# Decode block with attention and MLP in parallel: the last seven w2 rows in four column groups, and one add at the end

## The chip, the cores and the metric

The kernel runs on one core of a Trainium2 chip. Such a core has five engines that run side by side: TensorE (PE in the profile; its weight loads are PEld), VectorE (DVE), ScalarE (ACT), GpSimd (POOL) and SyncE (SP), which here only issues DMAs. TensorE writes its results to PSUM, the engines copy them from there to SBUF, and 16 DMA engines move data between SBUF and the chip's main memory (HBM).

The metric is the time of one execution on the device, in microseconds (us). A kernel is run several times and the median counts.

## The reference

Two rows of x (B = 2, one token each, D = 576) are normalised once and go through two branches. Branch A is attention with a key and value cache, 32 query heads on 16 key heads, over the last 2,048 of 8,192 positions. Branch B is an MLP of width F = 4,608 with a squared ReLU. The output is the sum of x and the two.

```python
def _B_ref(x, w1, b1, w2, b2):
    h = jnp.einsum("bsd,df->bsf", x, w1) + b1
    zero = jnp.zeros_like(h)
    r = jnp.where(h > zero, h, zero)
    h = r * r
    out = jnp.einsum("bsf,fd->bsd", h, w2) + b2
    return out

x = A_x
xn = _layernorm(x, axis=-1)
return x + _A_ref(xn, A_k_cache, A_v_cache, A_wq, A_wo) + _B_ref(xn, B_w1, B_b1, B_w2, B_b2)
```

All inputs and the output (2 x 1 x 576) are bf16.

## The kernel before

All large loads go through SP's DMA queue, in the order in which the program issues them: keys and values of eight units (4 key heads of one batch row each), wq in between, then w1, wo in two halves, and at the end w2. The matmuls follow the loads. Per unit TensorE transposes the keys (L281), multiplies them with the queries (L296), and after the softmax multiplies the values (L333).

Everything that adds to the output is summed in one PSUM tile, out_ps, of 34 partitions x 288 columns in f32. Row b of columns 0 to 287 is on partition b, row b of columns 288 to 575 on partition 32 + b. The helper out_acc (L242) makes one contribution: two matmuls with the same 128x2 weights, one for each half, 288 columns each, which write partitions 0 to 1 and 32 to 33. So the two go to two column groups of TensorE's array. x, the bias b2, 64 matmuls of wo, and all rows of w2 go through out_acc.

The "rows" of w2 are chunks of 128 of the 4,608 values of h: a chunk of h (128x2) is the weight, and 128 rows of w2 (128 x 576) stream through. w2 comes in four groups. Groups 0, 1 and 2 have nine such chunks each and one load each. Group 3 has seven chunks (FT = 7) in one tile, loaded in pieces of four, two and one (the list W2P: `(3, 0, 4), (3, 4, 6), (3, 6, 7)`); the rest of that group is in two small tiles loaded early on ACT's queue (w2x_sb, w2y_sb) and done by mlp_x. The function mlp_o(g, r0, r1) runs one entry of W2P.

The order at the end of the program is: values of the last units, wo_sel(1) and wo_acc(1) with the second half of wo, then the six entries of W2P, and then the end proper, which is L502 to L506: DVE casts columns 0 to 143 of out_ps to bf16, ACT columns 144 to 287 (both on 34 partitions), and SP's and ACT's queues each store one half of the columns of both rows, as two pieces of 576 bytes.

The first MLP layer (mlp_h_block, L377) and the query projection (q_block, L259) already use four column groups: the four matmuls of a chunk write partitions 32 g and 32 g + 1 for g = 0 to 3, with `tile_position=(0, 32 * g)`.

PSUM tiles are taken from rings. The ring misc has two buffers and serves, at the end of the program, oT_ps of the last unit, then wps of wo_sel(1). The tile framework puts in the waits between engines from the tiles that they read and write.

Of the kernel before, what the change touches and what calls it, by code (L numbers as in the profile page):

```python
# [8 lines left out]
F32 = mybir.dt.float32  # L9
BF16 = mybir.dt.bfloat16  # L10
ACT = mybir.ActivationFunctionType
ALU = mybir.AluOpType
# [4 lines left out]
def kernel(  # L17
# [14 lines left out]
    nc = tc.nc  # L32
    P = 128
    B, Sq, D = A_x.shape
# [27 lines left out]
    NG4 = 4  # L62
# [5 lines left out]
    FR = HW // P  # L68
    XR, XP, XE = 12, 20, 5
    FT = (HW - XR * XP) // P  # L70
# [6 lines left out]
    NFC = N3 + len(CX)  # L77
    RB = 32 * (NG4 - 1) + B
    OH = D // 2
    NP = NQ // 2  # L80
    WR = 2 * NC * Dh // P
    DW = Dh // WR
# [2 lines left out]
    const = ctx.enter_context(tc.tile_pool(name="const", bufs=1))  # L85
# [5 lines left out]
    work = ctx.enter_context(tc.tile_pool(name="work", bufs=2))  # L91
    keep = ctx.enter_context(tc.tile_pool(name="keep", bufs=3))
    psum = ctx.enter_context(tc.tile_pool(name="psum", bufs=1, space=bass.MemoryType.PSUM))

    x2d = A_x.rearrange("b s d -> (b s) d")
    out2d = out.rearrange("b s d -> (b s) d")

    k_tiles, v_tiles, wq_tiles, w1_tiles, wo_tiles, w2_tiles = {}, {}, {}, {}, {}, {}
# [135 lines left out]
    with nc.allow_low_precision(reason="sums of one 1 and zeros"):  # L234
        nc.vector.tensor_reduce(out=rmask[:], in_=ident[:].rearrange("p (c r) -> p r c", r=WR), axis=AX.X, op=ALU.add)
        nc.vector.tensor_reduce(out=sel[:, MZ:MZ + DW], in_=ident[:].rearrange("p (c r) -> p c r", r=WR), axis=AX.X,
                                op=ALU.add)

    out_ps = psum.tile([32 + B, OH], F32, tag="out", name="out_ps")
    nc.vector.memset(out_ps[:], 0.0)  # L240

    def out_acc(lhsT, rhs_of, start=False, stop=False, pin=False):  # L242
        for i in range(2):
            mm = nc.tensor.matmul(out_ps[32 * i:32 * i + B, :], lhsT=lhsT, rhs=rhs_of(i * OH, (i + 1) * OH),  # L244
                                  start=start, stop=stop, skip_group_check=True)
            if pin:
                tc.keep_in_program_order(mm)
# [111 lines left out]
    def wo_acc(tq):  # L359
        ws = wo_state.pop(tq)  # L360
        wo_sb = wo_tiles.pop(tq)
        for r in range(WR):
            out_acc(ws[:, r, :], lambda a, z: wo_sb[:, r, a:z])

    mlp = {}
# [36 lines left out]
            nc.vector.tensor_copy(out=hT_sb[0:m, N3 + i0:N3 + i1, :], in_=hb[0:m, i0:i1, :])  # L402
        mlp["h"] = hT_sb

    def mlp_o(g, r0, r1, last=False):
        w2_sb = w2_tiles.pop((g, r0))
        for r in range(r0, r1):
            o = (r - r0) * D
            out_acc(mlp["h"][:, g * FR + r, :], lambda a, z: w2_sb[:, o + a:o + z], stop=(last and r == r1 - 1))

    def mlp_x():
        for i, (c0, st, m) in enumerate(CX[FT:]):
# [15 lines left out]
    W2P = [(0, 0, 9), (1, 0, 9), (2, 0, 9), (3, 0, 4), (3, 4, 6), (3, 6, 7)]  # L428
# [23 lines left out]
    for g in range(NG):  # L452
# [7 lines left out]
                          in_=ident[0:NG4, 0:NG4].unsqueeze(2).to_broadcast([NG4, NG4, 32]))  # L460
# [34 lines left out]
        pv(NU - 1, g)  # L495
    wo_sel(1)
    wo_acc(1)
    for i in range(len(W2P)):
        mlp_o(*W2P[i], last=(i == len(W2P) - 1))

    fin_sb = work.tile([32 + B, OH], BF16, tag="fin", name="fin_sb")
    half_o = OH // 2  # L502
    nc.vector.tensor_copy(out=fin_sb[:, 0:half_o], in_=out_ps[:, 0:half_o])  # L503
    nc.scalar.copy(out=fin_sb[:, half_o:OH], in_=out_ps[:, half_o:OH])  # L504
    nc.sync.dma_start(out=out2d[:, 0:OH], in_=fin_sb[0:B, :])
    nc.scalar.dma_start(out=out2d[:, OH:D], in_=fin_sb[32:32 + B, :])  # L506


# [28 lines left out]
```

## Time and profile before

| | |
|---|---|
| median of 8 runs | 136.34 us (136.1 to 137.03) |
| the profiled execution, its own time | 137.03 us |
| its span, first to last instruction | 135.24 us |
| mean granted TensorE clock | 0.785 |
| busy share of the span | PE 76%, PEld 64%, DVE 42%, ACT 33%, POOL 5% |
| HBM read | 53.62 MB, 397 GB/s over the span |
| out_ps matmuls on w2 (L244), 128x288 | 68, of 386 ns mean |
| last casts (L503 DVE, L504 ACT), 34x144 | 300 ns and 273 ns |
| output stores (L505, L506) | 2, of 1.1 KB each |

The first rows of the profile give shares of the whole span. The matmuls' durations overlap, since several are in flight at once; their pace is the distance between their starts. The clock that the profile calls granted is a share of TensorE's full clock and changes during a run, between 0.5 and 1.0 here. A chain of waits follows the work that ended last back through whatever released it. L-numbers are lines of the kernel before.

### The profile page before, as it was taken

The numbers are of one execution on the slowest core, as the hardware profiler recorded it, in microseconds if no ns is written. First come the engines' busy times: TensorE is split into PE (matmuls) and PEld (weight loads), VectorE is DVE, ScalarE is ACT, GpSimd is POOL, SyncE is SP. The second block draws the span as 40 slices with busy tenths as digits, with TensorE's granted clock in tenths as the row PEclk, the third lists the DMA queues.
The fourth block names the chain that finished last, engine by engine and source line by source line (L and its number), as shares of the span: only waits on it lengthen the run. The fifth ranks groups of instructions, "written<-read, shape, count | busy, mean of one in ns | idle before, by whom it ended". The sixth has DMA issues, their size and how long they took to land.

```text
span 135.2 us, 4107 instructions
## 1 busy us (share of the span) xinstructions
PE 103.0 (76%) x1876; PEld 85.9 (64%) x1876; DVE 56.5 (42%) x133; ACT 44.4 (33%) x52; POOL 6.7 (5%) x21
## 2 busy tenths in 40 slices
PE   1072994786998689967979996998948999489491
PEld 0061471686987589867968995984417987445240
DVE  7631030455377358665564457247042456300000
ACT  6723020645466226454253315411040551000000
POOL 1000000011011011011010011011000001100000
PEclk9999999868699855999955555595599599555959
DMA  4999999999999999999999999999999999999930
GB/s 156 426 408 437 429 426 427 422 436 419 435 417 431 409 414 426 422 426 422 431 422 429 419 431 430 420 419 427 413 433 426 426 428 424 415 410 415 382 143 1
DMA packets 4430, 53.87 MB, mean 398 GB/s; under 512 B 527, under 2 KB 678, under 8 KB 1194
## 3 DMA queue, kind: packets, MB, share of 16 engines
q1 hardware_dynamic: 4324, 53.32, 93.6%
q8 instruction: 14, 0.23, 0.7%
q10 hardware_dynamic: 90, 0.31, 0.6%
q14 instruction: 2, 0.02, 0.0%
HBM read 53.62 MB, written 0.00 MB: 397 GB/s over the span
## 4 chain that ended last, share of the span: by engine, by line
PE 36%; DMA 36%; DVE 16%; ACT 4%; POOL 3%; issue 2%; SPq 1%; POOLq 0%; ACTq 0%
DMA w<-in_B_w_dram 23%; PE kT_ps L281 16%; DMA wq<-in_A_wq_dram 9%; PE sc_ps L296 7%; PE out_ps L244 6%; PE oT_ps L333 4%; DMA b_sb<-in_B_b_dram 4%; DVE l L315 3%; DVE sub L310 3%; DVE kT L286 3%; DVE m L302 3%; ACT pT L313 2%; PE q_ps L259 2%; ACT kT L284 2%; POOL gmax L306 1%
## 5 line engine op out<-in xcount | busy, mean ns | idle before, releaser
L281 PE MATMUL kT_ps<-ident,k 128*128 128x128 bf16 x512 | 51.4, 272 | 4.0 <-DVE kT L286 2.5
L281 PEld LDWEIGHTS <-k 128*128 128x128 bf16 x512 | 42.0, 124 | 5.5 <-issue 2.4
L284 ACT COPY kT<-kT_ps 128x1024 bf16<-128x1024 bf16 x32 | 31.8, 1011 | 36.8 <-PE kT_ps L281 35.3
L286 DVE COPY kT<-kT_ps 128x1024 bf16<-128x1024 bf16 x32 | 21.5, 682 | 27.1 <-PE kT_ps L281 26.6
L296 PE MATMUL sc_ps<-qT_all,kT 128*128 128x8 bf16 x512 | 22.1, 169 | 6.5 <-ACT kT L284 3.8
L296 PEld LDWEIGHTS <-kT 128*128 128x128 bf16 x512 | 20.1, 103 | 8.8 <-ACT kT L284 4.9
L333 PE MATMUL oT_ps<-pT,v 128*128 128x8 bf16 x512 | 15.3, 167 | 1.7 <-issue 1.2
L333 PEld LDWEIGHTS <-v 128*128 128x128 bf16 x512 | 14.2, 97 | 2.7 <-issue 2.1
L313 ACT ACTIVATE pT<-sub 128x512 bf16<-128x512 f32 x8 | 5.0, 631 | 20.1 <-DVE sub L310 20.1
L315 DVE TENSOR_REDUCE l<-pT 128x8 f32<-128x512 bf16 x8 | 8.6, 1069 | 3.7 <-ACT pT L313 3.6
L244 PE MATMUL out_ps<-wo,ws 128*2 128x288 bf16 x64 | 8.0, 442 | 1.3 <-DMA wo<-in_A_wo_dram 0.7
L244 PE MATMUL out_ps<-w,hT_sb 128*2 128x288 bf16 x68 | 7.2, 386 | 2.1 <-DMA w<-in_B_w_dram 2.1
L244 PEld LDWEIGHTS <-hT_sb 128*2 128x2 bf16 (+2 forms) x94 | 5.0, 102 | 5.8 <-issue 2.6
L302 DVE TENSOR_REDUCE m<-sc_ps 128x8 f32<-128x512 f32 x8 | 5.5, 692 | 5.4 <-PE sc_ps L296 5.4
L306 POOL PARTITION_ALL_REDUCE gmax<-m x8 | 3.0, 374 | 85.4 <-DVE m L304 85.4
L244 PEld LDWEIGHTS <-ws 128*2 128x2 bf16 x64 | 3.9, 121 | 4.5 <-DVE ws L356 1.2
L504 ACT CAST fin_sb<-out_ps 34x144 bf16<-34x144 f32 x1 | 0.3, 273 | 18.7 <-DVE fin_sb L503 18.7
L503 DVE CAST fin_sb<-out_ps 34x144 bf16<-34x144 f32 x1 | 0.3, 300 | 13.6 <-PE out_ps L244 13.6
L310 DVE TENSOR_TENSOR sub<-sc_ps,gm 128x512 f32<-128x512 f32 x8 | 5.5, 691 | 0.3
L259 PE MATMUL q_ps<-wq,xnT 128*2 128x512 bf16 x32 | 3.4, 482 | 3.0 <-DMA wq<-in_A_wq_dram 3.0
L317 POOL PARTITION_ALL_REDUCE lsum<-l x8 | 3.2, 399 | 23.2 <-DVE l L315 23.2
L387 DVE TENSOR_TENSOR hrow<-t 98x384 bf16<-98x384 f32 x3 | 1.6, 556 | 5.2 <-ACT t L386 5.0
(70 smaller groups left out, 43.8 us busy)
## 6 DMA issues: line engine op xcount, KB each, us to landing
k<-in_A_k_cache_dram SPq DMA_DIRECT2D x8, 2048.0 KB, 12.2
v<-in_A_v_cache_dram SPq DMA_DIRECT2D x8, 2048.0 KB, 25.0
wo<-in_A_wo_dram SPq DMA_DIRECT2D x2, 2304.0 KB
w<-in_B_w_dram SPq DMA_DIRECT2D x2, 2304.0 KB, 32.7
wq<-in_A_wq_dram SPq DMA_DIRECT2D x2, 2048.0 KB, 16.9
w<-in_B_w_dram SPq DMA_DIRECT2D x3, 1296.0 KB, 28.1
w_rem<-in_B_w_dram SPq DMA_DIRECT2D x1, 576.0 KB
w<-in_B_w_dram SPq DMA_DIRECT2D x1, 576.0 KB
```

Of the source, the lines that this page charges most:

```text
L244: mm = nc.tensor.matmul(out_ps[32 * i:32 * i + B, :], lhsT=lhsT, rhs=rhs_of(i * OH, (i + 1) * OH), start=start, stop=stop, skip_group_chec ...
L259: nc.tensor.matmul(q_ps[k][32 * g:32 * g + B, :], lhsT=xnT[:, xc, :], rhs=rhs, start=(c == 0), stop=(c == KC - 1), skip_group_check=True, ...
L281: nc.tensor.transpose(out=kT_ps[:, i * P:(i + 1) * P], in_=k_sb[:, j * Dh:(j + 1) * Dh], identity=ident[:])
L284: nc.scalar.copy(out=kT[:], in_=kT_ps[:])
L286: nc.vector.tensor_copy(out=kT[:], in_=kT_ps[:])
L296: nc.tensor.matmul(sc_ps[:, g * JG + i, :], lhsT=kT[:, i * P:(i + 1) * P], rhs=qT_all[:, b, tq * NC:(tq + 1) * NC], start=True, stop=True)
L302: nc.vector.tensor_reduce(out=m1[:], in_=sc_ps[:].rearrange("p j c -> p c j"), axis=AX.X, op=ALU.max)
L306: nc.gpsimd.partition_all_reduce(gmax[:], m2[:], channels=P, reduce_op=ReduceOp.max)
L310: nc.vector.tensor_tensor(out=sub[:], in0=sc_ps[:], in1=gm2[:].unsqueeze(1).to_broadcast([P, NJ, NC]), op=ALU.subtract)
L313: nc.scalar.activation(out=pT[:], in_=sub[:], func=ACT.Exp, scale=scale)
L315: nc.vector.tensor_reduce(out=l1[:], in_=pT[:].rearrange("p j c -> p c j"), axis=AX.X, op=ALU.add)
L333: nc.tensor.matmul(oT_ps[:], lhsT=v_sb[:, j * Dh:(j + 1) * Dh], rhs=pT_tiles[u][:, j, :], start=(j == 0), stop=(j == NJ - 1))
```

## The change

The first 27 chunks of w2 (groups 0 to 2) still go to out_ps. When the last of them is in, out_ps is copied to an f32 tile in SBUF, part, by four copies of 2x144, two by DVE and two by ACT, that also rearrange it: quarter i of the 576 columns goes to partitions 32 i and 32 i + 1. The last seven chunks go, by four matmuls of 144 columns each, to a new PSUM tile, tail_ps, with the same arrangement, in four column groups. At the end one DVE operation adds tail_ps and part on 98 partitions and writes bf16; the two stores then take one output row each, from four partitions that are 32 apart, in four pieces of 288 bytes.

part is zeroed by POOL at the start; tail_ps takes a buffer of the ring misc and is zeroed by DVE, which the program issues between the last use of DVE in wo_sel(1) and its cast of wps (L356). W2P, the loads and their order are as before.

```diff
+    OQ = D // 4
...
-    def mlp_o(g, r0, r1, last=False):
+    def mlp_o(g, r0, r1):
         w2_sb = w2_tiles.pop((g, r0))
         for r in range(r0, r1):
             o = (r - r0) * D
-            out_acc(mlp["h"][:, g * FR + r, :], lambda a, z: w2_sb[:, o + a:o + z], stop=(last and r == r1 - 1))
+            out_acc(mlp["h"][:, g * FR + r, :], lambda a, z: w2_sb[:, o + a:o + z], stop=(g == NG4 - 2 and r == r1 - 1))
+
+    part = const.tile([RB, OQ], F32, name="part")
+    nc.gpsimd.memset(part[:], 0.0)
+
+    def mlp_tail(r0, r1):
+        w2_sb = w2_tiles.pop((NG4 - 1, r0))
+        if r0 == 0:
+            mlp["out"] = psum.tile([P, OQ], F32, tag="misc", bufs=2, name="tail_ps")
+            nc.vector.memset(mlp["out"][:], 0.0)
+        for r in range(r0, r1):
+            o = (r - r0) * D
+            for i in range(4):
+                nc.tensor.matmul(mlp["out"][32 * i:32 * i + B, :], lhsT=mlp["h"][:, (NG4 - 1) * FR + r, :],
+                                 rhs=w2_sb[:, o + i * OQ:o + (i + 1) * OQ], start=(r == 0), stop=(r == FT - 1),
+                                 skip_group_check=True, tile_position=(0, 32 * i))
...
-    for i in range(len(W2P)):
-        mlp_o(*W2P[i], last=(i == len(W2P) - 1))
-
-    fin_sb = work.tile([32 + B, OH], BF16, tag="fin", name="fin_sb")
-    half_o = OH // 2
-    nc.vector.tensor_copy(out=fin_sb[:, 0:half_o], in_=out_ps[:, 0:half_o])
-    nc.scalar.copy(out=fin_sb[:, half_o:OH], in_=out_ps[:, half_o:OH])
-    nc.sync.dma_start(out=out2d[:, 0:OH], in_=fin_sb[0:B, :])
-    nc.scalar.dma_start(out=out2d[:, OH:D], in_=fin_sb[32:32 + B, :])
+    for w in W2P[:NG4 - 1]:
+        mlp_o(*w)
+    for i in range(4):
+        cp = nc.scalar.copy if i % 2 else nc.vector.tensor_copy
+        cp(out=part[32 * i:32 * i + B, :],
+           in_=out_ps[32 * (i // 2):32 * (i // 2) + B, (i % 2) * OQ:(i % 2 + 1) * OQ])
+    for w in W2P[NG4 - 1:]:
+        mlp_tail(*w[1:])
+
+    fin_sb = work.tile([RB, OQ], BF16, tag="fin", name="fin_sb")
+    nc.vector.tensor_tensor(out=fin_sb[:], in0=mlp["out"][0:RB, :], in1=part[:], op=ALU.add)
+    for b, eng in ((0, nc.sync), (1, nc.scalar)):
+        eng.dma_start(out=out2d[b:b + 1, :].rearrange("o (q n) -> (o q) n", q=4), in_=fin_sb[b:RB:32, :])
```

## The prediction

> **What bounds the kernel now.** I read the slices first, then the DMA share of the queues, then the chain of waits near its end, then the tail's instructions in order of time, then busy time and granted clock by stretch. The slices and the queue list say that the loads set the pace:
>
> ```profile
> PEclk9999999868699855999955555595599599555959
> DMA  4999999999999999999999999999999999999930
> q1 hardware_dynamic: 4324, 53.32, 93.6%
> ```
>
> The DMA row is at nine tenths or more in all but the first and the last two slices. So nothing before the last load can gain anything here; only what comes after the last weights can. The chain of waits shows what that is:
>
> ```profile
> 97.97 30.77 DMA w<-in_B_w_dram
> 128.74 0.04 issue
> 128.78 3.68 PE out_ps L244 x32
> 132.47 0.02 issue
> 132.49 0.31 DVE fin_sb L503
> 132.80 0.02 issue
> 132.82 0.27 ACT fin_sb L504
> ```
>
> One releasing load, then 32 matmuls (16 rows of w2, two each), then two casts one after the other, then the stores. The 16 rows are the nine of w2's third block (its load is the 1.89 us wait below) and the last seven, so the change touches 14 of these 32 matmuls, both casts and both stores. The tail in order of time (start, duration, then the instruction; each line is the first of a narrow window):
>
> ```profile
> 128.78 0.64 PE L244 MATMUL out_ps<-w,hT_sb 128*2 128x288 bf16 x4 [1.89 <-DMA w<-in_B_w_dram]
> 130.65 1.17 PE L244 MATMUL out_ps<-w,hT_sb 128*2 128x288 bf16 x8
> 132.03 0.41 PE L244 MATMUL out_ps<-w,hT_sb 128*2 128x288 bf16 x4
> 133.12 0.33 SPq L505 DMA_DIRECT2D out_dram<-fin_sb  x1
> 128.50:131.90 3.40, 3.12 (x28) 1.70 (x29) 0.00 (x0) 0.00 (x0) 0.00 (x0) 0.51 0.37 143
> 131.90:135.20 3.30, 0.54 (x8) 0.17 (x4) 0.30 (x1) 0.27 (x1) 0.00 (x0) 0.99 0.00 1
> ```
>
> The last two lines are stretches (busy time by engine, then granted clock, DMA share, GB/s): the clock is 0.51 until 131.9 and 0.99 after. In the half-clock part a row starts every 0.24 us, both of its matmuls within 5 ns of each other (288 columns, so 0.83 ns a column, two column groups side by side); at full clock every 0.12 us. The ninth row starts at 130.65, the tail's first at 130.89. The last packet of the last load ends at 130.80 in the packet records.
>
> **The change, part by part.** I count from 130.65 to the moment the stores are issued, now 133.12.
>
> *Tail matmuls.* Removed: 14 of 288 columns, in two groups. Added: 28 of 144 columns, in four groups, each with its weight load. The nearest row is the four-group matmul of the first MLP layer (L377, 128x384), which the trace has at both clocks: at half clock the same group starts again every 0.32 us, which is 384 x 0.83 ns, so four groups run as fast as one; at full clock every 0.16 us. By that a tail row takes 144 x 0.83 = 0.12 us. The floor of issue is lower: L296 (8 columns, a new weight load each) runs at 26.5 ns for a pair of load and matmul at half clock, so four pairs are 0.106 us. The upper bound is one group at a time: 4 x 0.12 = 0.48 us. I take 0.12, as the same form of instruction did it. The seventh row then starts at 130.89 + 6 x 0.12 = 131.61, after its load has landed (130.80), and a matmul lasts 0.444 - 0.24 + 0.12 = 0.324 us, so TensorE ends at 131.94 in place of 132.44.
>
> [...]
>
> *The copies out of out_ps.* These are new: four of 2x144, two on DVE and two on ACT, behind the ninth row's end at 130.65 + 0.444 = 131.10. The rows for them are the casts of 34x144: 0.300 us (DVE L503) and 0.273 us (ACT L504). In the changed program DVE's two copies wait for TensorE alone, while each ACT copy waits for the DVE copy of the same PSUM partitions, as the ACT cast does now. So with a hop of 0.02 to 0.03 us: DVE 131.13 to 131.43 and to 131.73; ACT 131.46 to 131.73 and 131.76 to 132.03. They lie beside the tail matmuls, in another PSUM tile; what of them is not covered is 132.03 - 131.94 = 0.09 us, so they, not TensorE, end last before the add, narrowly. Were all four in a row, they would end at 132.36.
>
> *The last operation.* Two casts in series (0.31 + 0.02 + 0.27 = 0.60 us) go; one DVE add of 98x144 comes, PSUM plus SBUF in f32 to bf16. The rows: the same operation on PSUM and SBUF takes 0.167 us for 8 columns (L338) and 0.691 for 512 (L310), 1.04 ns a column, so 0.31 us for 144. It starts at 132.06, ends at 132.37, and the stores are issued at 132.40: **0.72 us before** 133.12.
>
> *Stores.* Each goes from two pieces of 576 B to four of 288 B; still one on SP's queue and one on ACT's, nothing queued behind either. The present packets last 0.033 to 0.035 us each, the first starting 0.74 us after the issue and the last ending at 133.93; the rest to 135.24 is completion and the program's end. No packet between 88 and 576 B is in the trace. From below: 0.02 us less for a shorter packet. From above: one more trip of the length from issue to first data, 0.74 us, were a small piece read before it is written. I take zero, as the packets are a thirtieth of the 2.1 us and the rest does not depend on their size, and keep 0.74 for the range. [...]
>
> *At no cost.* The memset of part on POOL follows that of sel (128x248, 0.306 us, at 0.72) and has until POOL's first reduction, some 25 us later. The memset of tail_ps (at most 0.30 us by L240, 34x288) comes on DVE between L347, which ends at 118.20, and L356, which starts at 118.70 after waiting 0.49 us for wps. Without that cover ws would be up to 0.3 us later, and TensorE then still waits for wo's load (0.67 us of idle, to 119.33). Its buffer's last reader (L338, 117.58) is done. The 28 added TensorE instructions and 2 on DVE come at the end of their streams and push nothing else.
>
> **Sum.** In the profiled execution 137.03 - 0.72 = 136.31, of which the span is 135.24 and 1.79 lies around it. That execution is the slowest of the eight; the median, 136.34, is 0.69 below, and I subtract 0.7 from it: **135.64**. The difference of the two may be profiling, or clock. So I redo the sum with the clock: with the ninth row's start as zero, a tail all at half clock issues its stores at 7 x 0.24 + 0.444 + 0.68 = 2.80 now and 0.444 + 1.31 = 1.75 after, a gain of 1.05; one all at full clock at 0.84 + 0.287 + 0.68 = 1.81 now and 0.287 + 1.31 = 1.60 after, a gain of 0.2. The half-clock stretch began after the 1.89 us idle, which the median execution has too, so I stay with the mixed case and take these two as the likeliest case's own range: 135.3 to 136.14.
>
> **The rivals.**
> - *A warm tail.* Where the clock is full for the last rows, the matmuls saved are worth half as much and the copies, not TensorE, set the add. Gain 0.2 to 0.4, so 135.95 to 136.14. For it: the median is faster than the profiled execution, and full clock already came at 131.9. Against: the idle time ahead of it.
> - *The small stores pay another trip*: 135.64 + 0.74 = 136.38, no change. For it: no such packet is in the trace. Against: two packets of 576 B show no sign of a cost by size.
> - *The column groups do not run side by side for such short matmuls* (slower). The place is the seven tail rows. At 0.48 us a row the fourth matmul of the last row starts at 130.89 + 6 x 0.48 + 0.36 = 134.13 and ends at 134.45, the stores go at 134.81, 1.69 us later than now: 138.0. It decides from the pace at which the add would end where the casts end now, at 133.09: TensorE at 132.75, so 6.75 r + 0.324 = 1.86 after 130.89, r = 0.23 us a row. For it: four weight loads in 0.12 us have no row with a stream this short (a load lasts 0.126 us at half clock). Against: L377 overlaps the loads of all four groups with the streams.
> - *The edit changes nothing*, because the copies come late in their queues: in the changed program they stand directly behind ws on DVE and the last exp on ACT, both idle since before 120, so I give it nothing of its own.
>
> **How the numbers follow.** A measurement of this kernel tells about 0.3% (0.41 us) from no change. The forecast with a gain above 0.41 has 0.62; the warm tail 0.18, within 0.41; the stores 0.12, two thirds within 0.41 and the rest slower, where a warm tail adds to them; the serial groups 0.08, slower. So faster 0.62, same 0.26, slower 0.12. The range 135.3 to 136.4 takes in the forecast, the warm tail and the stores' plain case, and leaves out the serial groups, the part of the stores' case that is slower, and a little below.
>
> **What would show it.** Right: tail matmuls that start again in their group every 0.12 us at half clock, the last one ending some 0.8 us after the ninth row's; DVE copies of 0.30 us beside them; the add waiting for ACT's second copy, by under 0.1 us, and lasting 0.31 us; stores 1.7 us after the ninth row's start; 2.1 us from there to the end. Wrong: an add that waits for TensorE with a tail pace above 0.2 us, copies all in a row, or more than 2.3 us from issue to end. The prediction falls if the stores' end grows by over 0.7 us, or the clock in the tail is full in most executions.

## The result and the profile after

The changed kernel takes 135.48 us (median of 22 runs, 135.23 to 136.39) against 136.26 us (60 runs): a ratio of 0.9941, 95% interval 0.9927 to 0.9955, so 0.78 us faster. The forecast was 135.64. The time is right, and the working that led to it is mostly not, as the profile already hints. The profiled execution took 135.54 us, and its span is 133.6. First the same rows of the page as before: granted clock, DMA share, and the queue of the large loads.

```profile
PEclk9999999855699955999959959955955589658997
DMA  4999999999999999999999999999999999999950
q1 hardware_dynamic: 4328, 53.32, 94.2%
```

The same 53.32 MB arrive, but the share of the span is larger. The end of the chain of waits:

```profile
107.92 22.21 DMA w<-in_B_w_dram
130.14 0.04 issue
130.18 0.26 PE tail_ps L423 x4
130.44 0.03 issue
130.47 0.02 DVEq L524
130.49 0.04 issue
130.53 0.31 DVE fin_sb L524
```

Here the chain waits for the *last* load, and a single row (four matmuls) is left after it. Before, it waited for the load of w2's third block and did 16 rows after it. The tail in order of time, with what ended the idle time in brackets:

```profile
127.74 1.27 PE L245 MATMUL out_ps<-w,hT_sb 128*2 128x288 bf16 x18 [1.84 <-DMA w<-in_B_w_dram]
129.04 0.63 DVE L518 COPY part<-out_ps 2x144 f32<-2x144 f32 x2 [10.81 <-PE out_ps L245]
129.12 0.42 PE L423 MATMUL tail_ps<-w,hT_sb 128*2 128x144 bf16 x16
129.43 0.56 ACT L518 COPY part<-out_ps 2x144 f32<-2x144 f32 x2 [15.37 <-DVE part L518]
129.82 0.59 PE L423 MATMUL tail_ps<-w,hT_sb 128*2 128x144 bf16 x12 [0.28 <-DMA w<-in_B_w_dram]
130.53 0.31 DVE L524 TENSOR_TENSOR fin_sb<-tail_ps,part 98x144 bf16<-98x144 f32 x1 [0.86 <-PE tail_ps L423]
130.87 0.66 SPq L526 DMA_DIRECT2D out_dram<-fin_sb  x1
130.88 0.59 ACTq L526 DMA_DIRECT2D out_dram<-fin_sb  x1
127.00:130.20 3.20, 2.00 (x46) 1.21 (x45) 0.60 (x2) 0.54 (x2) 0.00 (x0) 1.00 0.53 210
```

Three readings differ from the forecast. The tail ran at full clock (1.00 in the stretch of the last line, third number from the end), nine rows of w2 in 1.27 us, and then waited for loads. The two stores take twice as long to issue, 0.66 and 0.59 us in place of 0.33 and 0.26. And everything is about a microsecond earlier: the nine rows start at 127.74, not 128.78. Since their start is the end of a load, that last point has nothing to do with the tail. The load stream itself is faster, which stretches of the run show (the last two columns are the DMA engines' share and GB/s). Before:

```profile
30.00:60.00 30.00, 25.38 (x576) 24.53 (x576) 17.78 (x35) 14.10 (x17) 2.30 (x6) 0.83 1.01 423
90.00:120.00 30.00, 24.15 (x487) 18.89 (x488) 12.08 (x31) 6.67 (x9) 1.53 (x4) 0.74 1.00 421
```

After:

```profile
30.00:60.00 30.00, 25.47 (x576) 24.55 (x576) 17.87 (x35) 14.12 (x17) 2.30 (x6) 0.79 1.01 429
90.00:120.00 30.00, 24.00 (x429) 18.12 (x427) 10.08 (x25) 6.04 (x8) 1.17 (x3) 0.67 1.00 426
```

The share is full in both, so no gap was closed; the same busy engines move about 1% more. In the packet records the last load packet ends at 129.78 after and at 130.79 before.

### The profile page after: what moved, and what is told of

Same layout as the page of the kernel before. It is cut to its first block, busy times and chain, and to the rows that moved or that the text cites. A ratio compares the mean times of both kernels' runs of the same rounds, so it can differ in the third digit from the quotient of the medians.

```text
span 133.6 us, 4142 instructions
## 1 busy us (share of the span) xinstructions
PE 97.7 (73%) x1890; PEld 81.7 (61%) x1890; DVE 57.3 (43%) x136; ACT 44.7 (33%) x53; POOL 6.8 (5%) x22
## 3 DMA queue, kind: packets, MB, share of 16 engines
q1 hardware_dynamic: 4328, 53.32, 94.2%
## 4 chain that ended last, share of the span: by engine, by line
DMA 57%; PE 21%; DVE 11%; ACT 3%; issue 2%; POOL 2%; SPq 0%; POOLq 0%; ACTq 0%; DVEq 0%
DMA v<-in_A_v_cache_dram 28%; DMA w<-in_B_w_dram 17%; PE kT_ps L282 11%; DMA wq<-in_A_wq_dram 9%; PE sc_ps L297 5%; DMA b_sb<-in_B_b_dram 4%; PE oT_ps L334 2%; DVE kT L287 2%; ACT kT L285 2%; DVE m L303 2%; DVE sub L311 2%; PE q_ps L260 2%; DVE l L316 2%; POOL gmax L307 1%; ACT pT L314 1%
## 5 line engine op out<-in xcount | busy, mean ns | idle before, releaser
L282 PE MATMUL kT_ps<-ident,k 128*128 128x128 bf16 x512 | 48.3, 261 | 3.6 <-DVE kT L287 2.2
L282 PEld LDWEIGHTS <-k 128*128 128x128 bf16 x512 | 39.8, 119 | 5.0 <-issue 2.1
L297 PEld LDWEIGHTS <-kT 128*128 128x128 bf16 x512 | 19.1, 100 | 9.4 <-ACT kT L285 4.9
L245 PEld LDWEIGHTS <-hT_sb 128*2 128x2 bf16 (+2 forms) x80 | 3.3, 82 | 5.2 <-issue 3.8
L245 PE MATMUL out_ps<-w,hT_sb 128*2 128x288 bf16 x54 | 3.8, 285 | 3.4 <-DMA w<-in_B_w_dram 3.4
L518 ACT COPY part<-out_ps 2x144 f32<-2x144 f32 x2 | 0.5, 268 | 15.4 <-DVE part L518 15.4
L378 PE MATMUL h_ps<-w,xnT 128*2 128x384 bf16 x48 | 3.9, 432 | 2.2 <-DMA w<-in_B_w_dram 2.2
L518 DVE COPY part<-out_ps 2x144 f32<-2x144 f32 x2 | 0.6, 299 | 10.8 <-PE out_ps L245 10.8
```

Source lines behind the costliest of these rows:

```text
L282: nc.tensor.transpose(out=kT_ps[:, i * P:(i + 1) * P], in_=k_sb[:, j * Dh:(j + 1) * Dh], identity=ident[:])
L297: nc.tensor.matmul(sc_ps[:, g * JG + i, :], lhsT=kT[:, i * P:(i + 1) * P], rhs=qT_all[:, b, tq * NC:(tq + 1) * NC], start=True, stop=True)
```

## The experiments

All ratios are to the kernel before, run on the same chip in the same session. There were three sessions, with medians of the kernel before of 136.27 us (b_again to tail2), 136.63 (b_pad64 to a_4stores) and 136.27 (b_pad128 to b_al_side), so medians of different sessions are compared with their ratios beside them. "Load end" is the end of the last load packet, in us from the span's start.

### The kernel before once more, and where the stores' time comes from

The first four runs ask whether the first profile's tail is the usual one, and what makes the stores dearer.

**b_again**: the kernel before, unchanged.

> The kernel before, unchanged, for a second profile of it. Theory A (the first profile, 137.03 us, was an execution with a half clock in the tail, and the usual execution of 136.2 has a full clock there): the chain of waits ends with the last w2 load, one or two rows after it, two casts of 0.3 us and the stores; stores issued about 0.7 us after the seventh row's start; span about 134.4. Theory B (the usual execution looks like the first profile): a tail at clock 0.5, all 32 matmuls after the 1.9 us wait on the chain, span 135.2. Time ratio 1.000 in both.

Measured: 136.42 us, ratio 1.0015 (0.9995 to 1.0034). Its chain and two stretches (clock third from the end):

```profile
130.27 0.04 issue
130.31 1.86 PE out_ps L244 x14
132.18 0.02 issue
127.00:130.20 3.20, 1.29 (x20) 0.78 (x18) 0.00 (x0) 0.00 (x0) 0.00 (x0) 1.00 0.77 307
130.20:132.20 2.00, 1.84 (x14) 0.81 (x13) 0.00 (x0) 0.00 (x0) 0.00 (x0) 0.50 0.11 39
```

Neither theory as written. The first nine rows ran at full clock here, the last seven at half. The clock in the tail differs from execution to execution of one program: over the first nine rows 0.50 in the first profile and 1.00 here. What does not differ is the load end, 130.94 here and 130.79 in the first profile, and that is 1.0 to 1.2 us later than in the changed kernel.

**b_step32**: the stores alone, in the kernel before.

```diff
-    nc.sync.dma_start(out=out2d[:, 0:OH], in_=fin_sb[0:B, :])
-    nc.scalar.dma_start(out=out2d[:, OH:D], in_=fin_sb[32:32 + B, :])
+    for b, eng in ((0, nc.sync), (1, nc.scalar)):
+        eng.dma_start(out=out2d[b:b + 1, :].rearrange("o (q n) -> (o q) n", q=2), in_=fin_sb[b:32 + B:32, :])
```

> Before, with each store taking one output row from two partitions 32 apart (two pieces of 576 B) instead of one column half from two neighbouring partitions (also two pieces of 576 B). Theory A (the form with partitions 32 apart makes the issue of a store 0.33 us longer and the way from issue to the end 0.6 us longer): issues of 0.66 and 0.59 us, first packet 1.2 us after the issue, 136.85 us, ratio 1.004. Rival B (the number or the size of the pieces does it, four of 288 B): issues of 0.33 and 0.26 us, first packet 0.74 us after the issue, ratio 1.000. Rival C (the longer issue in the changed kernel was chance): as B.

**a_adjacent**: the changed kernel with the step removed. It stores mostly zeros in place of the sums.

```diff
-        eng.dma_start(out=out2d[b:b + 1, :].rearrange("o (q n) -> (o q) n", q=4), in_=fin_sb[b:RB:32, :])
+        eng.dma_start(out=out2d[b:b + 1, :].rearrange("o (q n) -> (o q) n", q=4), in_=fin_sb[32 * b:32 * b + 4, :])
```

> The changed kernel, with each store taking its four pieces of 288 B from four neighbouring partitions instead of four that are 32 apart; so the stores bring other data than the sums (most of them are the zeros beside them), and all else is as in the changed kernel. Theory A (partitions 32 apart cost 0.6 us): issues of 0.33 and 0.26 us, 2.1 us from issue to end, 134.9 us, ratio to before 0.990. Rival B (four pieces of 288 B cost it): issues of 0.66 and 0.59 us, 2.7 us from issue to end, 135.5 us, ratio 0.994.

Measured: b_step32 136.92 us, ratio 1.0054 (1.0042 to 1.0067); a_adjacent 135.05 us, ratio 0.9912 (0.9898 to 0.9925). The stores of b_step32 (two pieces of 576 B from partitions 32 apart), in order of time:

```profile
132.40 0.64 SPq L506 DMA_DIRECT2D out_dram<-fin_sb  x1
132.40 0.59 ACTq L506 DMA_DIRECT2D out_dram<-fin_sb  x1
```

And those of a_adjacent (four pieces of 288 B from neighbouring partitions):

```profile
130.91 0.34 SPq L526 DMA_DIRECT2D out_dram<-fin_sb  x1
130.92 0.28 ACTq L526 DMA_DIRECT2D out_dram<-fin_sb  x1
```

From the first issue to the span's end it is 2.12 us before, 2.74 in the changed kernel, 2.68 in b_step32 and 2.20 in a_adjacent. So it is the step of 32 partitions that costs; the number and the size of the pieces make 0.08 us. The issue itself takes 0.33 us longer with the step. In the packet records, the first packet of the later of the two queues leaves 0.79 us after its issue before, 1.41 in b_step32 and 1.51 in the changed kernel.

**tail2**: a part of the change, with the old two groups and the old stores.

```diff
+            for i in range(2):
+                nc.tensor.matmul(mlp["out"][32 * i:32 * i + B, :], lhsT=mlp["h"][:, (NG4 - 1) * FR + r, :],
+                                 rhs=w2_sb[:, o + i * OH:o + (i + 1) * OH], start=(r == 0), stop=(r == FT - 1),
...
+    nc.vector.tensor_copy(out=part[0:B, :], in_=out_ps[0:B, :])
+    nc.scalar.copy(out=part[32:32 + B, :], in_=out_ps[32:32 + B, :])
...
+    nc.vector.tensor_tensor(out=fin_sb[:], in0=mlp["out"][0:32 + B, :], in1=part[:], op=ALU.add)
+    nc.sync.dma_start(out=out2d[:, 0:OH], in_=fin_sb[0:B, :])
+    nc.scalar.dma_start(out=out2d[:, OH:D], in_=fin_sb[32:32 + B, :])
```

> Part of the change alone: the last seven rows go to a PSUM tile of their own, in two groups of 288 columns as before, the sum of the rest leaves PSUM ahead of them (DVE and ACT one half each, side by side), one add of 34x288 (0.46 us) ends it, and the stores are those of before. Theory A (usual executions have a full clock in the tail and wait for the last load, so the four groups bring nearly nothing, the one operation instead of two brings 0.15 us, and the old stores are 0.6 us cheaper than the new): 135.1 us after a full-clock tail, about 0.4 below the changed kernel; ratio 0.991. But by the saved casts alone it should be only 0.15 below before: 136.1, ratio 0.999; so if the gain of the changed kernel came from casts and groups in spite of its dearer stores, this run tells how much of it the early leaving alone brings. Rival B (the four groups bring the gain): 0.15 us below before or less, ratio 0.998 to 1.000.

Measured: 135.99 us, ratio 0.9975 (0.9960 to 0.9989). The gain is smaller than theory A's 0.991 although the tail ran at full clock (nine rows in 1.27 us, as in the changed kernel), and near rival B's figure. But its load end is 130.76, not 129.78, which neither theory had foreseen: the two kernels with the early load end have four groups, so either the groups or something that goes with them moves the loads.

### What moves the loads

No load, buffer or order differs between before and after. What differs is where the buffers lie. The new tile part takes 576 bytes of each partition ahead of the pools for keys, values and weights. In the program's allocation the first key buffer starts at byte 42,944 before and 43,520 after. The other load buffers move with it and keep the same place within 256 bytes: 192 past a multiple of 256 before, a multiple of 512 after. In tail2 part is 1,152 bytes, and the place is 64. Three of the next four runs test this; the fourth, a_4stores, goes on with the stores.

**b_pad64**: the kernel before, moved.

```diff
+    pad = const.tile([RB, 16], F32, name="pad")
+    nc.gpsimd.memset(pad[:], 0.0)
```

> The kernel before, with one more tile of 64 bytes per partition, written once by POOL at the start and never read, in the place where the change allocates part. It moves the destinations of all large loads in SBUF from 192 bytes past a multiple of 256 to a multiple of 512, where part (576 bytes) puts them in the changed kernel; no instruction of the computation is changed. Theory A (most of the change's gain is this move: the loads end 1.0 us earlier in the two changed kernels seen, 129.8 against 130.8 to 130.9, and their 10368-byte packets take 390 ns against 398): last load packet ends at 129.8 to 129.9, 135.25 us, ratio 0.9925. Theory B (the early leaving and the four groups bring the gain, and the earlier end of the loads follows from them or is chance): ratio 1.000.

**a_pad448**: the changed kernel, moved back, with the same two lines and `[RB, 112]`.

> The changed kernel with one more unread tile of 448 bytes per partition, so that the loads' destinations are again 192 bytes past a multiple of 256, as before. Theory A: the last load ends at 130.8, and what is left of the change is the shorter tail less the dearer stores: 136.4 us, ratio 1.001. Theory B: unchanged against the changed kernel, 135.5 us, ratio 0.994.

Measured: b_pad64 135.16 us, ratio 0.9889 (0.9862 to 0.9916), load end 129.76; a_pad448 136.70 us, ratio 1.0008 (0.9989 to 1.0026), load end 130.98. Stretches of b_pad64:

```profile
30.00:60.00 30.00, 25.41 (x584) 24.45 (x585) 17.43 (x34) 13.80 (x17) 2.29 (x6) 0.83 1.01 427
90.00:120.00 30.00, 25.11 (x509) 19.83 (x508) 12.28 (x31) 6.67 (x9) 1.52 (x4) 0.73 1.01 428
```

And of a_pad448:

```profile
30.00:60.00 30.00, 25.39 (x576) 24.47 (x576) 18.00 (x35) 14.38 (x16) 2.29 (x6) 0.79 1.00 421
90.00:120.00 30.00, 23.04 (x421) 17.21 (x419) 10.09 (x25) 6.04 (x8) 1.16 (x3) 0.73 1.00 423
```

Theory A held in both. The old computation in the new place has the fast loads, and the new computation in the old place has the slow ones. The move alone brings the whole gain and more. The change without the move brings nothing that can be measured.

**tail2_al**: tail2 at multiples of 512. Here part shares the memory of hrow, and the unread tile of 64 bytes moves the loads.

> The earlier run with two groups of 288, the early leaving, one add of 34x288 and the stores of before, now with the loads' destinations at multiples of 512 (part shares the memory of hrow, and an unread tile of 64 bytes moves the loads). Theory A (move 1.0 us, early leaving and one operation 0.3 us, both add up): 135.0 us, ratio 0.990, about 0.45 us below the changed kernel. Theory B (the move brings nothing by itself): 136.0 us, ratio 0.9975.

**a_4stores**: the changed kernel with stores without the step.

```diff
-    for b, eng in ((0, nc.sync), (1, nc.scalar)):
-        eng.dma_start(out=out2d[b:b + 1, :].rearrange("o (q n) -> (o q) n", q=4), in_=fin_sb[b:RB:32, :])
+    for q in range(4):
+        (nc.sync if q < 2 else nc.scalar).dma_start(out=out2d[:, q * OQ:(q + 1) * OQ], in_=fin_sb[32 * q:32 * q + B, :])
```

> The changed kernel with four stores of two neighbouring partitions each (two pieces of 288 B; two stores on SP's queue, two on ACT's) in place of two stores from partitions 32 apart. If the step of 32 alone is dear: issues of 0.33 and 0.27 us, two in a row per queue, 2.4 us from the first issue to the end in place of 2.74, 135.2 us, ratio 0.992. If the second issue on a queue costs as much as the step saves: 135.5 us, ratio 0.994.

Measured: tail2_al 135.00 us, ratio 0.9892 (0.9860 to 0.9925); a_4stores 135.27 us, ratio 0.9902 (0.9872 to 0.9932). tail2_al matches theory A, but its gain over b_pad64 lies within the intervals, and the spans are 133.14 and 133.19. a_4stores took 2.58 us from the first issue to the end, against 2.4 expected and 2.74 in the changed kernel:

```profile
130.88 0.64 SPq L526 DMA_DIRECT2D out_dram<-fin_sb  x2
130.88 0.57 ACTq L526 DMA_DIRECT2D out_dram<-fin_sb  x2
```

Two plain issues in a row occupy a queue as long as one with the step: 0.64 and 0.57 us, against 0.66 and 0.59.

### Which place counts

**b_pad128**, **b_pad192**, **b_pad320**: b_pad64 with other sizes of the unread tile.

> The kernel before with an unread tile of 128 bytes: destinations of the large loads 64 bytes past a multiple of 256. Theory A (what counts is a multiple of 256): loads end at 130.8, 136.2 us, ratio 1.000. Theory B (what counts is a multiple of 64, or any move does it): no more to gain than now, since 192 is a multiple of 64 too, ratio 1.000. Theory C (the address moves the time by something else than its place in 256, as the size of the added tile): 135.2 us, ratio 0.990. The partial change with a tile of 1152 bytes had this place (64) and its loads ended at 130.76.

> The kernel before with an unread tile of 192 bytes: destinations 128 bytes past a multiple of 256. Theory A (a multiple of 256 counts): loads end at 130.8, ratio 1.000. Theory C (a multiple of 128 is enough): 129.8, 135.2 us, ratio 0.990.

> The kernel before with an unread tile of 320 bytes: destinations at a multiple of 256 that is none of 512. Theory A (a multiple of 256 counts): loads end at 129.8, 135.2 us, ratio 0.990. Theory C (a multiple of 512 is needed): loads end at 130.8, ratio 1.000.

Measured: b_pad128 135.98 us, ratio 0.9967 (0.9948 to 0.9987); b_pad192 135.98 us, ratio 0.9972 (0.9960 to 0.9985); b_pad320 134.94 us, ratio 0.9895 (0.9870 to 0.9919). A multiple of 256 is enough. The added tile and its memset are in b_pad128 and b_pad192 as well, so they do not bring the 1 us by themselves. And 64 and 128 past it are 0.3 us better than 192, which no theory had. The packet records of all 14 profiles fall into the same three classes (packet times are medians in ns by size in bytes; the last column is the summed packet time of the load queue per DMA engine):

```
place mod 256   kernels                               load end          16384  18432  10368   us per engine
192             before, b_again, b_step32, a_pad448   130.79 to 130.98  613    688    398     126.5 to 126.8
64, 128         tail2, b_pad128, b_pad192             130.65 to 130.76  613    688    389     126.5
0               after, a_adjacent, a_4stores,         129.72 to 129.90  611    686    389     125.6 to 125.9
                tail2_al, b_pad64, b_pad320, b_al_side
```

(Medians are within 1 ns in each class.) The 10368-byte packets, those of w2's first three blocks, are slow at 192 only. The large ones are faster at 0 only. On average the packets of an engine take 126.7 us at 192 and 125.8 at 0, a difference of 0.9 us, and the loads end at 130.9 and 129.8, a difference of 1.1; where the remaining 0.2 lies is open. The means differ by more than the medians: a packet of 16,384 bytes takes 622 to 624 ns on average at 192 and 617 to 620 at 0, and with 145 such packets per engine this makes 0.6 of the 0.9 us.

tail2 and b_pad128 have the same place, and 135.99 and 135.98 us. So tail2's ratio of 0.9975 was the move too, not rival B, and the early leaving with one add brings nothing visible.

**b_al_side**: the kernel of b_pad64, and the casts side by side.

```diff
-    nc.vector.tensor_copy(out=fin_sb[:, 0:half_o], in_=out_ps[:, 0:half_o])
-    nc.scalar.copy(out=fin_sb[:, half_o:OH], in_=out_ps[:, half_o:OH])
+    nc.vector.tensor_copy(out=fin_sb[0:B, :], in_=out_ps[0:B, :])
+    nc.scalar.copy(out=fin_sb[32:32 + B, :], in_=out_ps[32:32 + B, :])
```

> The kernel before with the unread tile of 64 bytes (loads at multiples of 512), and the last casts split by output half instead of by column: DVE casts partitions 0 and 1, ACT partitions 32 and 33, 288 columns each, so that neither waits for the other and each store waits for one of them. By the part copies of the same size (0.446 us DVE, 0.39 us ACT) against 0.60 us for the two casts in a row: 0.15 us below the aligned kernel, 135.0 us, ratio 0.989; the ACT store goes out 0.06 us ahead of the other. If the two still wait for each other: 0.2 us above it, 135.4 us.

Measured: 134.90 us, ratio 0.9900 (0.9871 to 0.9929). The casts in order of time:

```profile
130.54 0.45 DVE L505 CAST fin_sb<-out_ps 2x288 bf16<-2x288 f32 x1 [12.28 <-PE out_ps L244]
130.57 0.39 ACT L506 CAST fin_sb<-out_ps 2x288 bf16<-2x288 f32 x1 [16.32 <-PE out_ps L244]
130.99 0.27 ACTq L508 DMA_DIRECT2D out_dram<-fin_sb  x1
131.01 0.33 SPq L507 DMA_DIRECT2D out_dram<-fin_sb  x1
```

Neither waits for the other, and the first store goes 0.45 us after the casts began. The time cannot be told from that of b_pad64. All kernels at a multiple of 256 with the old stores, 134.90 to 135.16 us (ratios 0.9889 to 0.9900), have medians below the changed kernel's 135.48 (0.9941).

## Why the prediction was right in its number and wrong in its reason

*"So nothing before the last load can gain anything here; only what comes after the last weights can."* This is the step that failed. It took the duration of the loads as given, and listed part as a memset of 0.3 us on POOL, "at no cost". The memset cost nothing (0.218 us at 1.0 us), but the tile's 576 bytes moved every large load buffer to a multiple of 512, and the loads ended 1.0 us earlier. b_pad64 and a_pad448 show that this is where the gain comes from. Two of the prediction's own signs of being wrong came true as well: more than 2.3 us from issue to end (2.74), and a full clock in the tail of most profiled executions (12 of 14).

*The tail matmuls.* The mechanism was right: four groups side by side, rows 0.06 us apart at full clock (16 matmuls in 0.42 us with their drain), half of the 0.12 forecast at half clock. The rival with serial groups is out. But the place was wrong: I made the sum in a tail that TensorE sets, with the clock of one execution. The prediction expected the half clock to come back because it began after the wait of 1.89 us; b_again has a wait of 1.91 us at the same place, and its clock behind it is 1.00. With a full clock the tail waits for its loads piece by piece (the idle ahead of 129.82 above, and another ahead of the last row at 130.18), and what the groups save is spent in waiting. The "warm tail" was written as a rival with a gain of 0.2 to 0.4; it is the state of 12 of the 14 profiles, all but the two of the kernel before.

*Copies and add.* Sizes right: 0.296 to 0.302 and 0.268 us for the copies (0.300 and 0.273), 0.308 for the add (0.31), and the copies alternate as said. They did not end last before the add, though: they were done at 129.99, and the add waited for TensorE. The hop from TensorE to the add was 0.12 us (end 130.41, start 130.535), in place of 0.02 to 0.03. By the program the add needs two engines, TensorE's tail_ps and ACT's last copy into part, and in the chain an instruction of DVE's queue (the DVEq line) stands ahead of it. In b_pad64 the cast needs TensorE alone, no such line stands there, and the hop is 0.04 us (130.40 to 130.44). That the second wait is the reason is inferred. Against b_pad64, the same place with the old tail, the stores go out at 130.87 in place of 131.07, 1.09 and 1.31 us after the load end: a direct gain of 0.2 us. The line of b_pad64:

```profile
131.07 0.32 SPq L508 DMA_DIRECT2D out_dram<-fin_sb  x1
```

*Stores.* Taken at zero, measured 0.62 us. The upper bound of 0.74 held it, but for the wrong cause: piece size, where it was the partition step. This term was mis-sized by the most among those of the sum. In a_adjacent four pieces of 288 B cost 0.08 us more than two of 576 B (2.20 us from issue to end, against 2.12). That a small piece is read before it is written, on which the upper bound rested, no run shows. (The prediction has the last packet of before end at 133.93; that is its start, and it ends at 133.96.)

*The sum.* Forecast: 0.72 from the tail and nothing else. Measured, after against b_again: 1.16 from the load end, 0.17 from what follows it (4.01 to 3.84), which is a faster clock, the shorter end and the dearer stores together. The direct parts, 0.2 gained and 0.62 lost, come to a loss of 0.4 us at equal place and full clock: in the profiles 3.84 us from load end to span end against 3.43 for b_pad64, and 135.48 against 135.16 in the medians (ratios 0.9941 and 0.9889). At the old place a_pad448 lost only 0.0008 of the time (0.9989 to 1.0026). The profiles there fit a tail of before that runs at half clock in some executions, where the shorter tail is worth more. From load end to span end, before and b_again, with a half clock in the tail, take 4.44 and 4.01 us. b_step32, at full clock, takes 4.15, which is 3.59 without the 0.56 that its stores cost. a_pad448 takes 3.93. No run fixed the clock, so how often each case occurs is open. So it is luck that 135.64 and 135.48 agree: two errors offset each other, 1.0 us of loads that I had not seen, against 0.6 us of stores and 0.5 us of a tail gain that is 0.2 and not 0.72. The three measured parts, 1.0 + 0.2 - 0.6, come to 0.6 us of the 0.78; which part has the other 0.2 is open.

Why the place counts was not shown. Between 192 and 0 the median of a 10,368-byte packet differs by 2.3% (398 and 389 ns), and that of a 16,384-byte packet by 0.3% (613 and 611 ns; the mean by 0.7%). At 64 and 128 the 10,368-byte packets are as fast as at 0 (389 ns), and those of 16,384 bytes as slow as at 192 (613 ns). The tiles that the engines work on moved together with the load buffers, and no run moved one without the other.

## What to carry to other kernels

In a kernel whose loads fill the DMA engines all the time, look where the load buffers start: here a tile of 64 bytes ahead of them made the kernel before 1.1% faster (b_pad64, ratio 0.9889), and one of 448 bytes made the changed kernel 0.7% slower (a_pad448, 1.0008 in place of 0.9941). So when an edit adds or drops a tile, compare with a kernel that has the old code and the new addresses before crediting the edit. At the end of a kernel, count the issue of the last store with its access pattern, and prefer neighbouring partitions: here the step of 32 cost 0.3 us of issue and about 0.6 us to the end.

## What the runs showed of the hardware

- Loads to SBUF addresses at a multiple of 256 bytes ended 0.9 to 1.3 us earlier, of 130, than at 192 past it (129.72 to 129.90 against 130.79 to 130.98), and a multiple of 512 was no better than one of 256 (129.72 to 129.86 and 129.90).
- A store from partitions 32 apart took 0.59 to 0.66 us to issue against 0.26 to 0.34 from neighbours, and 0.56 to 0.63 us longer to the end than the store of before (2.68 to 2.75 against 2.12).
- The clock in the tail differed between executions of one program: in the two profiles of the kernel before, the first nine of the last 16 rows ran at half clock (a row every 0.24 us) and at full clock (every 0.12 us).
